# Wider weight-gradient chunks, whole spectral weights and another order of weight transfers in a fused spectral/SwiGLU forward-backward kernel

## Chip, cores and metric

The kernel runs on one core of one Trainium2 chip. The metric is device time in microseconds (us), lower is better. Times are medians over runs; traces are single profiled runs. The engines are called PE (TensorE), DVE (VectorE), ACT (ScalarE), POOL (GpSimd) and SP (SyncE). SP, POOL and ACT start transfers: I call their streams of transfers the sync queue, the software queue (POOL) and the ACT queue.

## The reference

One layer, forward and backward, in bf16 with x of 2048 x 512 (S x D) and F = 1792:

```python
def _A_ref(x, w_r, w_i):
    X = rfft2(x.astype(float32))            # 2048 x 257 complex
    return irfft2(X * (w_r + 1j * w_i), s=(S, D)).astype(bfloat16)

def _B_ref(x, w1, w3, w2):
    return (silu(x @ w1) * (x @ w3)) @ w2

def _fwd_reference(x, w_r, w_i, w1, w3, w2):
    h = x + _A_ref(_layernorm(x), w_r, w_i)
    return h + _B_ref(_layernorm(h), w1, w3, w2)
# outputs: the result, and the gradients of x, w_r, w_i, w1, w3, w2 for grad_out
```

## The kernel before

The transforms are matrix products with tables that the kernel makes itself. The order is: layernorm and the forward transform (`r_pass` with stages A, D, B, then `rt_pass`), eight FFN chunks, forward and backward fused, then the backward transform (`r_pass` over `gh_all`, `rt_pass`), and last the weight gradients (wgrad). A framework turns this text into one instruction order for each engine. It places wgrad matmuls as filler into gaps of the backward transform where buffers allow, and it lays out the memory.

Names used below: U is the buffer that carries a transform's result from stage D to stage B (psA, psD and psB are the matmul sums of its stages); `a` holds the FFN's hidden activations, `gg` and `gu` their gradients, and a_t and g_t are transposed chunks of them; go_all is the output gradient, hn_all the normalized rows; ga_ps and o_ps are sums of the FFN. A transfer lands when its data has arrived; time to landing counts from its issue.

The start, where most weights are transferred:

```python
fcp = wes.enter_context(tc.tile_pool(name="fcp", bufs=2))      # chunk buffers of the FFN
...
for pi in range(4):                                            # spectral weights, 2 of 16 rows each
    nc.gpsimd.dma_start(out=wr_c[:], in_=wr_v[:, 2 * pi:2 * pi + 2, :])
    nc.gpsimd.dma_start(out=wi_c[:], in_=wi_v[:, 2 * pi:2 * pi + 2, :])
nc.sync.dma_start_transpose(out=W['w2T'][:], in_=B_w2)
tmpw = gh_all[:, 0:NFB, :]
nc.sync.dma_start_transpose(out=tmpw, in_=B_w1)
nc.sync.dma_start(out=st['w1T'][:], in_=tmpw)
nc.sync.dma_start_transpose(out=tmpw, in_=B_w3)
nc.sync.dma_start(out=st['w3T'][:], in_=tmpw)
...
xn = sp.tile([P, J, D], BF16, name="xn", tag="bigB")           # U has the same tag: it waits
for hlf in range(2):                                           # until xn has been stored
    ...                                                        # layernorm of 8 of 16 rows
    nc.sync.dma_start(out=st['xn'][:, sl, :], in_=xn[:, sl, :])
...
nc.gpsimd.dma_start(out=W['w1'][:], in_=...)
nc.gpsimd.dma_start(out=W['w3'][:], in_=...)
```

The end: loads of the backward transform, and wgrad with chunks of 256 of the 1792 hidden columns:

```python
wpools = dict(big=tile_pool(name="wbig", bufs=3), res=tile_pool(name="wres", bufs=2),
              op=tile_pool(name="wop", bufs=3), ...)
def w_bwd(kl, br, bi):                                         # every second kl
    nc.gpsimd.dma_start(out=state['xs'][:], in_=st['X'][:, kl0:kl0 + 2, :, :])   # xs_c
    nc.gpsimd.dma_start(out=state['wr'][:], in_=wr_v[:, kl0:kl0 + 2, :])         # wr_c
    nc.gpsimd.dma_start(out=state['wi'][:], in_=wi_v[:, kl0:kl0 + 2, :])         # wi_c
...
def wgrad_phase(..., lq, sq):                                  # lq = nc.sync, sq = nc.gpsimd
    go_all = res.tile([P, J, D], BF16, name="go_all", tag="res")
    sq.dma_start(out=go_all[:], in_=go_v)                      # 2 MB
    for f0 in range(0, F, 256):
        a_t = big.tile([P, J, 256], BF16, name="a_t", tag="big")
        lq.dma_start_transpose(out=a_t[:], in_=st['a'][f0:f0 + 256, :])          # 1 MB
        ...                                                    # 2 x 16 matmuls 128x512, 2 outputs
    hn_all = res.tile([P, J, D], BF16, name="hn_all", tag="res")
    sq.dma_start(out=hn_all[:], in_=st['hn'][:])               # 2 MB
    for key, outw in (('gg', out4), ('gu', out5)):
        for f0 in range(0, F, 256):
            ...                                                # g_t 1 MB, 4 x 16 matmuls 128x256
```

## Time and profile before

| | before |
|---|---|
| time, first 4 runs | 729.88 us median (724.06 to 744.47) |
| time, all 16 runs beside the changed kernel | 739.21 us median (724.06 to 747.71) |
| span of the profiled run | 725.9 us |
| first matmul on U (stage B, forward) | 69.7 us |
| last FFN matmul | 474.8 us |
| last stage-B matmul of the backward transform | 529.6 us |
| last wgrad matmul | 719.8 us |

The profile page of before: busy time of PE in us, its share of the span and the number of its instructions, then some of its rows of 40 equal slices, in tenths of a slice.

```profile
PE 636.7 (88%) x4736; PEld 453.1 (62%) x4736; DVE 435.1 (60%) x1349; ACT 298.2 (41%) x585; POOL 77.0 (11%) x140
PE   0261999989989898999999899979999999999996
PEclk9995998999999999999999999999999999999999
DMA  9998320375506051331506050698510589988881
```

A slice is 18 us. After the fourth slice PE is near full to the end. So time can be won mainly where PE stands, in the first 70 us.

The timeline of before's sync queue (start, time in the queue, instruction):

```profile
1.70 32.53 SPq L610 DMA_TRANSPOSE w2T<-in_B_w_dram  x1
34.27 7.30 SPq L612 DMA_TRANSPOSE gh_all<-in_B_w_dram  x1
...
51.13 6.95 SPq L614 DMA_TRANSPOSE gh_all<-in_B_w_dram  x1
58.18 0.52 SPq L629 DMA_DIRECT2D st_xn<-xn  x1
...
60.59 0.76 SPq L629 DMA_DIRECT2D st_xn<-xn  x1
```

And what U waited for in before (the waits: who waits for what, us in total, times, longest):

```profile
DVE U L72 <- DMA st_xn<-xn: 23.0, 1, 23.0
...
PE psBr L213 <- ACT U L71: 17.8, 1, 17.8
```

The store of xn stands behind three transposes, U waits for the store, PE waits for U. The first transpose took 32.5 us, a later one of the same size 7.3 us.

### The profile page before, as it was taken

The numbers are of one execution on the slowest core, as the hardware profiler recorded it, in microseconds if no ns is written. First come the engines' busy times: TensorE is split into PE (matmuls) and PEld (weight loads), VectorE is DVE, ScalarE is ACT, GpSimd is POOL, SyncE is SP. The second block draws the span as 40 slices with busy tenths as digits, with TensorE's granted clock in tenths as the row PEclk, the third lists the DMA queues.
The fourth block names the chain that finished last, engine by engine and source line by source line (L and its number), as shares of the span: only waits on it lengthen the run. The fifth ranks groups of instructions, "written<-read, shape, count | busy, mean of one in ns | idle before, by whom it ended". The sixth has DMA issues, their size and how long they took to land.

```text
span 725.9 us, 12323 instructions
## 1 busy us (share of the span) xinstructions
PE 636.7 (88%) x4736; PEld 453.1 (62%) x4736; DVE 435.1 (60%) x1349; ACT 298.2 (41%) x585; POOL 77.0 (11%) x140
## 2 busy tenths in 40 slices
PE   0261999989989898999999899979999999999996
PEld 0141987467574746657574748559865444788885
DVE  6940787769393947759493957477986874010010
ACT  1560335566181634537181736354356552000000
POOL 4000310010000000000000000033410222111221
PEclk9995998999999999999999999999999999999999
DMA  9998320375506051331506050698510589988881
GB/s 255 226 280 296 98 79 1 111 244 203 163 30 182 30 167 31 107 90 62 150 31 181 31 166 3 177 252 332 142 50 29 121 189 212 230 178 196 171 193 37
DMA packets 167979, 103.87 MB, mean 143 GB/s; under 512 B 111600, under 2 KB 154608, under 8 KB 166896
## 3 DMA queue, kind: packets, MB, share of 16 engines
q1 hardware_dynamic: 159168, 68.43, 38.9%
q0 software_dynamic: 8464, 33.60, 14.2%
q10 hardware_dynamic: 288, 1.05, 0.4%
q8 instruction: 37, 0.61, 0.3%
q14 instruction: 22, 0.18, 0.1%
HBM read 29.91 MB, written 45.63 MB: 104 GB/s over the span
## 4 chain that ended last, share of the span: by engine, by line
DVE 30%; PE 23%; issue 17%; DMA 13%; SPq 10%; POOL 4%; ACT 2%; POOLq 0%; ACTq 0%; DVEq 0%
SPq L610 4%; DMA h_c<-st_h 4%; PE ps L278 3%; SPq L449 3%; DVE t L422 3%; POOL out_dram L492 3%; SPq L441 3%; DVE ggT L425 3%; DMA gh_all<-in_B_w_dram 3%; DVE aT L418 2%; DVE t L424 2%; DVE guT L426 2%; PE psDr L204 2%; PE psDi L205 2%; PE ghn_ps L446 2%
## 5 line engine op out<-in xcount | busy, mean ns | idle before, releaser
L485 PE MATMUL pw<-g_t,hn_all 128*128 128x256 bf16 x896 | 98.0, 273 | 0.0
L485 PEld LDWEIGHTS <-hn_all 128*128 128x128 bf16 x896 | 87.7, 98 | 10.4
L445 PE MATMUL ghn_ps<-w1T,ggT 128*128 128x512 bf16 x224 | 84.9, 379 | 0.0
L446 PE MATMUL ghn_ps<-w3T,guT 128*128 128x512 bf16 x224 | 84.9, 379 | 0.0
L409 PE MATMUL ga_ps<-goT,w2T 128*128 128x256 bf16 x448 | 67.2, 272 | 11.6 <-ACT th L415 11.6
L405 PE MATMUL g_ps<-hnT,w 128*128 128x256 bf16 x448 | 67.2, 273 | 1.9 <-DVE goT L388 1.9
L407 PE MATMUL u_ps<-hnT,w 128*128 128x256 bf16 x448 | 67.2, 273 | 0.0
L490 DVE CAST o_w<-pw 128x512 bf16<-128x512 f32 x14 | 9.7, 692 | 88.1 <-PE pw L485 88.1
L204 PE MATMUL psDr<-FD,Tt 128*128 128x257 bf16 x256 | 59.7, 279 | 2.1 <-ACT Tt L71 2.1
L205 PE MATMUL psDi<-FD,Tt 128*128 128x257 bf16 x256 | 59.6, 278 | 0.0
L437 PE MATMUL o_ps<-w,aT 128*128 128x512 bf16 x224 | 50.9, 379 | 7.3 <-DVE aT L418 7.3
L409 PEld LDWEIGHTS <-w2T 128*128 128x128 bf16 x448 | 43.8, 98 | 17.7 <-issue 12.7
L466 PE MATMUL pw<-go_all,a_t 128*128 128x512 bf16 x224 | 51.4, 379 | 0.0
L405 PEld LDWEIGHTS <-w 128*128 128x128 bf16 x448 | 43.8, 98 | 8.6 <-issue 2.0
L407 PEld LDWEIGHTS <-w 128*128 128x128 bf16 x448 | 43.8, 98 | 5.1
L488 ACT CAST o_w<-pw 128x512 bf16<-128x512 f32 x14 | 8.2, 585 | 89.6 <-PE pw L485 89.6
L307 DVE BATCH_NORM_STATS2 ln_st<-h_c 128x6 f32<-128x512 bf16 x16 | 10.4, 684 | 52.7 <-DMA h_c<-st_h 52.7
L437 PEld LDWEIGHTS <-aT 128*128 128x128 bf16 x224 | 21.0, 98 | 33.6 <-DVE aT L418 10.7
L191 PE MATMUL psA<-TT,xn 128*128 128x256 bf16 x64 | 11.5, 338 | 34.5 <-DVE xn L329 28.0
L414 ACT ACTIVATE sg<-g_ps 128x512 bf16<-128x512 f32 x56 | 34.7, 619 | 15.3 <-DVE guT L426 8.9
L345 ACT ACTIVATE lb_t<-lb_gsb,lb_ne,rinv_all 128x512 f32<-128x512 f32 x16 | 13.0, 813 | 64.4 <-DVE ln_t L315 34.7
L204 PEld LDWEIGHTS <-Tt 128*128 128x128 bf16 x256 | 37.1, 145 | 3.4 <-ACT Tt L71 2.3
(221 smaller groups left out, 1244.9 us busy)
## 6 DMA issues: line engine op xcount, KB each, us to landing
st_a<-aT SPq DMA_DIRECT2D x8, 896.0 KB, 4.7
st_gg<-ggT SPq DMA_DIRECT2D x8, 896.0 KB, 6.3
st_gu<-guT SPq DMA_DIRECT2D x8, 896.0 KB, 9.0
w<-in_B_w_dram POOLq DMA_DIRECT2D x3, 1792.0 KB, 19.6
out_dram<-o_w POOLq DMA_DIRECT2D x42, 128.0 KB, 3.6
wr_c<-in_A_w_r_dram POOLq DMA_DIRECT2D x16, 128.5 KB, 5.3
wi_c<-in_A_w_i_dram POOLq DMA_DIRECT2D x16, 128.5 KB, 4.0
st_X<-xs_t POOLq DMA_DIRECT2D x8, 257.0 KB, 2.5
```

Source lines behind the costliest of these rows:

```text
L204: nc.tensor.matmul(pr[:, :DF], lhsT=lhsT, rhs=T.FD[:, v_re, dc, :], start=(n == 0), stop=(n == 7))
L205: nc.tensor.matmul(pi[:, :DF], lhsT=lhsT, rhs=T.FD[:, v_im, dc, :], start=(n == 0), stop=(n == 7))
L405: nc.tensor.matmul(g_ps[:, fbi, :], lhsT=W['w1'][:, dc, fs], rhs=hnT[:, dc, :], start=(dc == 0), stop=(dc == 3))
L407: nc.tensor.matmul(u_ps[:, fbi, :], lhsT=W['w3'][:, dc, fs], rhs=hnT[:, dc, :], start=(dc == 0), stop=(dc == 3))
L409: nc.tensor.matmul(ga_ps[:, fbi, :], lhsT=W['w2T'][:, dc, fs], rhs=goT[:, dc, :], start=(dc == 0), stop=(dc == 3))
L414: nc.scalar.activation(out=sg[:], in_=g_ps[:], func=ACT.Silu)
L437: nc.tensor.matmul(o_ps[:], lhsT=aT[:, fb, jj * P:(jj + 1) * P], rhs=W['w2'][:, fb, :], start=(fb == 0), stop=(fb == NFB - 1))
L445: nc.tensor.matmul(ghn_ps[:], lhsT=ggT[:, fb, jj * P:(jj + 1) * P], rhs=W['w1T'][:, fb, :], start=(fb == 0), stop=False)
L446: nc.tensor.matmul(ghn_ps[:], lhsT=guT[:, fb, jj * P:(jj + 1) * P], rhs=W['w3T'][:, fb, :], start=False, stop=(fb == NFB - 1))
L466: nc.tensor.matmul(pw[:], lhsT=a_t[:, j, fbi * P:(fbi + 1) * P], rhs=go_all[:, j, :], start=(j == 0), stop=(j == J - 1))
L485: nc.tensor.matmul(pw[:, dd, :], lhsT=hn_all[:, j, db * P:(db + 1) * P], rhs=g_t[:, j, :], start=(j == 0), stop=(j == J - 1))
L610: nc.sync.dma_start_transpose(out=W['w2T'][:], in_=B_w2)
```

## The change

The intent: let the forward transform start sooner (xn stored before the third weight transpose, fewer and larger loads), and give wgrad fewer, wider steps (512 columns, chunks in four shared 2 MB slots instead of three 1 MB chunk slots and two 2 MB slots). Row-wise gx transfers and a separate pool for the first FFN chunk make the memory fit.

```diff
 def wgrad_phase(...):
-    FW = 256
-    go_all = res.tile([P, J, D], BF16, name="go_all", tag="res")
+    FCH = [(0, 512), (512, 512), (1024, 512), (1536, 256)]
+    go_all = big.tile([P, J, D], BF16, name="go_all", tag="big")
     sq.dma_start(out=go_all[:], in_=go_v)
-    for f0 in range(0, F, FW):
-        a_t = big.tile([P, J, FW], BF16, name="a_t", tag="big")
-        lq.dma_start_transpose(out=a_t[:], in_=st['a'][f0:f0 + FW, :])
+    for ci, (f0, fw) in enumerate(FCH):
+        a_t = big.tile([P, J, 512], BF16, name="a_t", tag="big")
+        lq.dma_start_transpose(out=a_t[:, :, :fw], in_=st['a'][f0:f0 + fw, :])
+        if ci == 1:
+            hn_all = big.tile([P, J, D], BF16, name="hn_all", tag="big")
+            sq.dma_start(out=hn_all[:], in_=st['hn'][:])
 ...                      # outputs in pairs: 23 transfers instead of 42
-    fcp = wes.enter_context(tc.tile_pool(name="fcp", bufs=2))
+    cp0 = wes.enter_context(tc.tile_pool(name="cp0", bufs=1))   # first chunk only; fcp later
 ...
-        for pi in range(4):  ...   # 8 loads of 2 rows, and 8 more later
+        nc.gpsimd.dma_start(out=wr_t[:], in_=wr_v)
+        nc.gpsimd.dma_start(out=wi_t[:], in_=wi_v)
 ...
-        nc.sync.dma_start_transpose(out=tmpw, in_=B_w3)
-        nc.sync.dma_start(out=st['w3T'][:], in_=tmpw)
 ...                      # layernorm, xn stores
+        nc.sync.dma_start_transpose(out=tmpw, in_=B_w3)
+        nc.sync.dma_start(out=st['w3T'][:], in_=tmpw)
+        nc.sync.dma_start(out=W['w1'][:], in_=...)
+        nc.sync.dma_start(out=W['w3'][:], in_=...)
-        nc.gpsimd.dma_start(out=W['w1'][:], in_=...)
-        nc.gpsimd.dma_start(out=W['w3'][:], in_=...)
 ...
-        wpools = dict(big=...bufs=3, res=...bufs=2, op=...bufs=3, ...)
+        wpools = dict(big=...bufs=4, op=...bufs=2, ...)
 ...                      # gx: xnr and gxt row by row; four xs buffers in the forward pass
```

More of the change, by code (lines that the diff above doesn't have):

```diff
@@ L452, in wgrad_phase @@
 def wgrad_phase(nc, grad_out, st, out4, out5, out6, pools, lq, sq):
-    big, res, op, ps = (pools[k] for k in ("big", "res", "op", "ps"))
+    big, op, ps = (pools[k] for k in ("big", "op", "ps"))
     go_v = grad_out.rearrange("(p j) d -> p j d", j=J)
-    FW = 256
+    FCH = [(0, 512), (512, 512), (1024, 512), (1536, 256)]
     k = 0
-    go_all = res.tile([P, J, D], BF16, name="go_all", tag="res")
-    sq.dma_start(out=go_all[:], in_=go_v)
-    for f0 in range(0, F, FW):
-        a_t = big.tile([P, J, FW], BF16, name="a_t", tag="big")
-        lq.dma_start_transpose(out=a_t[:], in_=st['a'][f0:f0 + FW, :])
-        for fbi in range(FW // P):
-            fb = f0 // P + fbi
-            pw = ps.tile([P, D], FP32, name="pw", tag="ps")
-            for j in range(J):
-                nc.tensor.matmul(pw[:], lhsT=a_t[:, j, fbi * P:(fbi + 1) * P], rhs=go_all[:, j, :], start=(j == 0), stop=(j == J - 1))
-            o = op.tile([P, D], BF16, name="o_w", tag="o")
-            if k % 2 == 0:
-                nc.scalar.copy(out=o[:], in_=pw[:])
-            else:
-                nc.vector.tensor_copy(out=o[:], in_=pw[:])
-            k += 1
-            sq.dma_start(out=out6[fb * P:(fb + 1) * P, :], in_=o[:])
@@ L474, in wgrad_phase, with evac @@
-    hn_all = res.tile([P, J, D], BF16, name="hn_all", tag="res")
-    sq.dma_start(out=hn_all[:], in_=st['hn'][:])
+    def evac(o_ap, p_ap):
+        nonlocal k
+        if k % 2 == 0:
+            nc.scalar.copy(out=o_ap, in_=p_ap)
+        else:
+            nc.vector.tensor_copy(out=o_ap, in_=p_ap)
+        k += 1
+    go_all = big.tile([P, J, D], BF16, name="go_all", tag="big")
+    sq.dma_start(out=go_all[:], in_=go_v)
+    hn_all = None
+    out6_v = out6.rearrange("(fb p) d -> p fb d", p=P)
@@ new lines, in wgrad_phase @@
+    for ci, (f0, fw) in enumerate(FCH):
[4 more added lines that the diff above has]
+            sq.dma_start(out=hn_all[:], in_=st['hn'][:])
+        nfb = fw // P
+        for fb2 in range(nfb // 2):
+            o = op.tile([P, 2, 512], BF16, name="o_w", tag="o")
+            for fbi in range(2):
+                fbl = fb2 * 2 + fbi
+                pw = ps.tile([P, D], FP32, name="pw", tag="ps")
+                for j in range(J):
+                    nc.tensor.matmul(pw[:], lhsT=a_t[:, j, fbl * P:(fbl + 1) * P], rhs=go_all[:, j, :], start=(j == 0), stop=(j == J - 1))
+                evac(o[:, fbi, :], pw[:])
+            fbg = f0 // P + fb2 * 2
+            sq.dma_start(out=out6_v[:, fbg:fbg + 2, :], in_=o[:])
@@ L476, in wgrad_phase @@
     for key, outw in (('gg', out4), ('gu', out5)):
-        for f0 in range(0, F, FW):
-            g_t = big.tile([P, J, FW], BF16, name="g_t", tag="big")
-            lq.dma_start_transpose(out=g_t[:], in_=st[key][f0:f0 + FW, :])
+        outw_v = outw.rearrange("(db p) f -> p db f", p=P)
+        for (f0, fw) in FCH:
+            g_t = big.tile([P, J, 512], BF16, name="g_t", tag="big")
+            lq.dma_start_transpose(out=g_t[:, :, :fw], in_=st[key][f0:f0 + fw, :])
             for db2 in range(2):
-                pw = ps.tile([P, 2, FW], FP32, name="pw1", tag="ps")
+                o = op.tile([P, 2, 512], BF16, name="o_w", tag="o")
@@ L482, in wgrad_phase @@
                 for dd in range(2):
                     db = db2 * 2 + dd
+                    pw = ps.tile([P, 512], FP32, name="pw1", tag="ps")
                     for j in range(J):
-                        nc.tensor.matmul(pw[:, dd, :], lhsT=hn_all[:, j, db * P:(db + 1) * P], rhs=g_t[:, j, :], start=(j == 0), stop=(j == J - 1))
-                o = op.tile([P, 2, FW], BF16, name="o_w", tag="o")
-                if k % 2 == 0:
-                    nc.scalar.copy(out=o[:], in_=pw[:])
-                else:
-                    nc.vector.tensor_copy(out=o[:], in_=pw[:])
@@ L491, in wgrad_phase @@
-                k += 1
-                sq.dma_start(out=outw[db2 * 2 * P:(db2 * 2 + 2) * P, f0:f0 + FW].rearrange("(dd p) f -> p dd f", p=P), in_=o[:])
+                        nc.tensor.matmul(pw[:, :fw], lhsT=hn_all[:, j, db * P:(db + 1) * P], rhs=g_t[:, j, :fw], start=(j == 0), stop=(j == J - 1))
+                    evac(o[:, dd, :fw], pw[:, :fw])
+                sq.dma_start(out=outw_v[:, db2 * 2:db2 * 2 + 2, f0:f0 + fw], in_=o[:, :, :fw])
 def bg_weight_transposes(nc, T, W, st, w2nat, psb, stg, dq):
@@ L602 @@
             eng.dma_start(out=xt[:, g4 * 4:(g4 + 1) * 4, :], in_=x_v[:, g4 * 4:(g4 + 1) * 4, :])
-        wch = []
-        for pi in range(4):
-            wr_c = s4.tile([P, 2, DF], BF16, name="wr_c", tag="wr_c")
-            wi_c = s4.tile([P, 2, DF], BF16, name="wi_c", tag="wi_c")
-            nc.gpsimd.dma_start(out=wr_c[:], in_=wr_v[:, 2 * pi:2 * pi + 2, :])
-            nc.gpsimd.dma_start(out=wi_c[:], in_=wi_v[:, 2 * pi:2 * pi + 2, :])
-            wch.append((wr_c, wi_c))
+        wr_t = sp.tile([P, J, DF], BF16, name="wr_t", tag="wr_t")
+        wi_t = sp.tile([P, J, DF], BF16, name="wi_t", tag="wi_t")
+        nc.gpsimd.dma_start(out=wr_t[:], in_=wr_v)
+        nc.gpsimd.dma_start(out=wi_t[:], in_=wi_v)
         nc.sync.dma_start_transpose(out=W['w2T'][:], in_=B_w2)
@@ L629 @@
             nc.sync.dma_start(out=st['xn'][:, sl, :], in_=xn[:, sl, :])
+        nc.sync.dma_start_transpose(out=tmpw, in_=B_w3)
+        nc.sync.dma_start(out=st['w3T'][:], in_=tmpw)
+        nc.sync.dma_start(out=W['w1'][:], in_=B_w1.rearrange("(dc p) f -> p dc f", p=P))
+        nc.sync.dma_start(out=W['w3'][:], in_=B_w3.rearrange("(dc p) f -> p dc f", p=P))
         scrB = sp.tile([P, 8192], I32, name="scrB", tag="bigA")
         gen_tables_FD_KB(nc, T, smc, scrB, io)
-        nc.gpsimd.dma_start(out=W['w1'][:], in_=B_w1.rearrange("(dc p) f -> p dc f", p=P))
-        nc.gpsimd.dma_start(out=W['w3'][:], in_=B_w3.rearrange("(dc p) f -> p dc f", p=P))
         Y = sp.tile([P, J, 2, DF], BF16, name="Y", tag="bigC")
@@ L641, in w_fwd @@
             if kk == 0:
-                state['xs'] = s2.tile([P, 2, 2, DF], BF16, name="xs_t", tag="xs_t")
-                if kl0 // 2 < len(wch):
-                    state['wr'], state['wi'] = wch[kl0 // 2]
-                else:
-                    state['wr'] = s4.tile([P, 2, DF], BF16, name="wr_c", tag="wr_c")
-                    state['wi'] = s4.tile([P, 2, DF], BF16, name="wi_c", tag="wi_c")
-                    nc.gpsimd.dma_start(out=state['wr'][:], in_=wr_v[:, kl0:kl0 + 2, :])
-                    nc.gpsimd.dma_start(out=state['wi'][:], in_=wi_v[:, kl0:kl0 + 2, :])
+                state['xs'] = s4.tile([P, 2, 2, DF], BF16, name="xs_t", tag="xs_t")
+                state['wr'] = wr_t[:, kl0:kl0 + 2, :]
+                state['wi'] = wi_t[:, kl0:kl0 + 2, :]
             xs = state['xs']
@@ L659, in w_fwd @@
                 t2 = s2.tile([P, 2, DF], BF16, name="wt2", tag="wt2")
-                nc.vector.tensor_tensor(out=t1[:], in0=Xr, in1=wr_c[:], op=ALU.mult)
-                nc.vector.tensor_tensor(out=t2[:], in0=Xi, in1=wi_c[:], op=ALU.mult)
+                nc.vector.tensor_tensor(out=t1[:], in0=Xr, in1=wr_c, op=ALU.mult)
+                nc.vector.tensor_tensor(out=t2[:], in0=Xi, in1=wi_c, op=ALU.mult)
                 nc.vector.tensor_tensor(out=Y[:, kl0:kl0 + 2, 0, :], in0=t1[:], in1=t2[:], op=ALU.subtract)
@@ L664, in w_fwd @@
                 t4 = s2.tile([P, 2, DF], BF16, name="wt2", tag="wt2")
-                nc.vector.tensor_tensor(out=t3[:], in0=Xr, in1=wi_c[:], op=ALU.mult)
-                nc.vector.tensor_tensor(out=t4[:], in0=Xi, in1=wr_c[:], op=ALU.mult)
+                nc.vector.tensor_tensor(out=t3[:], in0=Xr, in1=wi_c, op=ALU.mult)
+                nc.vector.tensor_tensor(out=t4[:], in0=Xi, in1=wr_c, op=ALU.mult)
                 nc.vector.tensor_tensor(out=Y[:, kl0:kl0 + 2, 1, :], in0=t3[:], in1=t4[:], op=ALU.add)
@@ L680, in h_cons @@
                 if j0 == 0:
-                    state['h0'] = fcp.tile([P, 2, D], BF16, name="h_c", tag="h_c")
+                    state['h0'] = cp0.tile([P, 2, D], BF16, name="h_c", tag="h_c")
                 state['ht'] = state['h0'] if j0 == 0 else s2.tile([P, 2, D], BF16, name="ht", tag="ht")
@@ L689 @@
         rt_pass(nc, T, Y, sp, ps, h_cons, Evac(nc), Evac(nc), Evac(nc))
-        ch = ffn_prologue(nc, T, st, half, go_v, 0, fcp, sm, s2, ps, rinv2_all, m2_all, h_src=state['h0'])
+        ch = ffn_prologue(nc, T, st, half, go_v, 0, cp0, sm, s2, ps, rinv2_all, m2_all, h_src=state['h0'])
     wpB = wes.enter_context(tc.tile_pool(name="wpB", bufs=1))
@@ L701 @@
         fsm = es.enter_context(tc.tile_pool(name="fsm", bufs=2))
+        fcp = es.enter_context(tc.tile_pool(name="fcp", bufs=2))
         ftp = es.enter_context(tc.tile_pool(name="ftp", bufs=2))
@@ L716 @@
     with ExitStack() as es:
-        wpools = dict(big=es.enter_context(tc.tile_pool(name="wbig", bufs=3)),
-                      res=es.enter_context(tc.tile_pool(name="wres", bufs=2)),
-                      op=es.enter_context(tc.tile_pool(name="wop", bufs=3)),
+        wpools = dict(big=es.enter_context(tc.tile_pool(name="wbig", bufs=4)),
+                      op=es.enter_context(tc.tile_pool(name="wop", bufs=2)),
                       ps=es.enter_context(tc.tile_pool(name="wps", bufs=2, space=PSUM)))
@@ L779, in gx_cons @@
                 j0 = j - jj
-                if jj == 0:
-                    state['xnr'] = s2.tile([P, 2, D], BF16, name="xnr", tag="xnr")
-                    nc.gpsimd.dma_start(out=state['xnr'][:], in_=st['xn'][:, j0:j0 + 2, :])
-                    state['gxt'] = s2.tile([P, 2, D], BF16, name="gxt", tag="gxt")
-                ln_bwd_row(nc, sm, fpool, pso[:], state['xnr'][:, jj, :], rinv1[:, j:j + 1], gh_all[:, j, :],
-                           state['gxt'][:, jj, :], use_pool=False)
-                if jj == 1:
-                    nc.gpsimd.dma_start(out=out1_v[:, j0:j0 + 2, :], in_=state['gxt'][:])
+                xnr = s4.tile([P, D], BF16, name="xnr", tag="xnr")
+                nc.gpsimd.dma_start(out=xnr[:], in_=st['xn'][:, j, :])
+                gxt = s2.tile([P, D], BF16, name="gxt", tag="gxt")
+                ln_bwd_row(nc, sm, fpool, pso[:], xnr[:], rinv1[:, j:j + 1], gh_all[:, j, :], gxt[:], use_pool=False)
+                nc.gpsimd.dma_start(out=out1_v[:, j, :], in_=gxt[:])
             rt_pass(nc, T, GX, sp, ps, gx_cons, Evac(nc), Evac(nc), Evac(nc))
```

## The prediction

> **What bounds the kernel now.** The span is 725.9 us. The table of stretches shows TensorE (PE) near full after 70 us: 100% busy at 70-100 us, 93-95% in the FFN (180-470 us), 100% at 540-718 us; but 15.6 us of the first 70. The wgrad phase is bound by matmul streaming: by the view of one source line, the w1/w3-gradient matmuls (128x256) come 94 in 10 us, 106 ns each; the w2-gradient ones (128x512) 48 in 10 us, 208 ns each. So 256 columns already stream at the full rate.
>
> The hole at the start waits for one buffer. The chain of waits shows the sync queue holding the w2 transpose (1.7-34.2 us), the w1 transpose (9.4), the w1T store (7.4), the w3 transpose (9.0), and only then the store of xn (8.6). U shares a buffer with xn, so its evictions wait for that store: by the waits, VectorE 23.0 us, PE 17.8 us. PE does two steps of stage D at 48.1-51.8 us, stands until 69.7 us, and comes back cold: matmuls last 0.42 us instead of 0.27 until 74.6 us, granted clock 0.5. The Trainium skill ("TensorE: Matmul & The Clock Gate", Part 1) says an idle array falls to half rate until about 3.4 us of sustained work; the trace agrees, 4.9 us here.
>
> **What the change does.**
> 1. The w3 transpose goes behind the xn stores. The w1/w3 loads (1.8 MB each, issued at 9.8-11.3 us beside the w2 transpose) follow it on the sync queue; the spectral weights come as two 1 MB loads. The w2 transpose took 32.5 us, the w1 one of the same size 7.3: contention, so I expect the w2 transpose done by 20-28 us. Then xn's second half, computed at 39.5 us, is stored by 46-50 us, and U is written from 49 us. PE does 320 matmuls at 0.11 us from 48.1 us and ends near 84 us instead of 104: about -20 us if the wait vanishes, -14 us if half a store stays; all on the critical path.
> 2. wgrad: 896 matmuls of 256 columns become 384 of 512 and 128 of 256; by the measured rates about the same time. Weight loads (98 ns) halve but were hidden.
> 3. Larger chunks cost a bubble. The four big slots hold the gradient, hn and two chunks; the first gg chunk gets its slot only when the third a chunk is used up. Its 2 MB transpose, estimated from the 1.83 MB one (9.4 us to landing), takes 10-12 us; the last a chunk gives PE only 32 x 0.21 = 6.8 us. PE stands 4-5 us, perhaps returning cold: +4 to +7 us. Later chunks have three slots and 13.6 us of work each.
> 4. Four xs buffers, row-wise gx transfers, the first FFN chunk's own pool, 23 output DMAs instead of 42: off the path, within 1 us.
>
> **Sum.** -19 + 5 = -14 us on a median of 729.88: about 715; I lean a little lower, 714, range 704 to 724. Faster by over 2% 0.57, within 2% 0.39, slower 0.04.
>
> **What would show it.** VectorE's wait for the xn store under 6 us; no PE hole at 52-69 us, no half clock at 70-75; the forward transform's end 14-20 us earlier; FFN chunks unchanged at 40.4 us; wgrad at 208 ns per 512 columns; one PE wait of 3-6 us before the first gg matmul.
>
> **What would make it wrong.** A scheduler orders each queue; it may still put the w3 transpose ahead of the xn store: then the gain is near 0. The w2 transpose may be slow by itself, so that the xn store leaves late. The bubble may be hidden if a chunks finish early as filler, or repeat if 2 MB transposes take over 13.6 us.

## The result, and the profile after

The changed kernel is correct and slower: 770.87 us median (762.38 to 778.42, 11 runs), against 739.21 us for before (16 runs). The ratio is 1.056, with a 95% interval of 1.049 to 1.064. A ratio is always the mean time of one kernel's fast runs over that of before's fast runs of the same rounds, so it isn't quite the ratio of the quoted medians. Most of before's own runs fall into two groups, 724 to 728 us and 736 to 748 us; some of the slower ones were sorted out as slow, depending on the fastest run of their batch. A ratio can therefore move by a per cent between batches, and I read no smaller difference across batches.

The page of the changed kernel, the same rows as before:

```profile
PE 641.4 (83%) x4352; PEld 417.2 (54%) x4352; DVE 434.2 (56%) x1351; ACT 298.7 (39%) x587; POOL 65.6 (9%) x121
PE   0279999849999989999999997009999999699897
PEclk9979999989999999999999999558999999899999
DMA  9992104825060605141423248997610286968941
```

PE's work is nearly the same (641.4 and 636.7 us), so the loss is standing time. There is a new hole of two slices (19 us each) near 490 us, in which the DMA row reads 9, and two new dips (at the ninth slice and near the end). The granted clock reads half (5) in the hole itself. Milestones, read from the traces, place the difference of the spans, 42.6 us (more than the 31.7 us between the medians, since before's trace is one of its quicker runs):

| event on PE | before, us | after, us | difference, summed | this step |
|---|---|---|---|---|
| first FFN matmul | 156.0 | 140.6 | -15.4 | -15.4 start |
| first o_ps matmul (first chunk's tail) | 175.2 | 174.4 | -0.8 | +14.6 first chunk |
| last FFN matmul | 474.8 | 468.0 | -6.8 | -6.0 given back in later chunks |
| last stage-B matmul, backward | 529.6 | 563.7 | +34.1 | +40.9 the hole |
| last a matmul | 621.8 | 654.7 | +32.9 | -1.2 |
| first gg matmul | 622.0 | 661.5 | +39.5 | +6.6 slot |
| last wgrad matmul | 719.8 | 763.2 | +43.4 | +3.9 output buffers |
| end | 725.9 | 768.5 | +42.6 | -0.8 |

The changed kernel's waits, the lines that answer to those of before and the new ones of PE:

```profile
DVE U L72 <- DMA st_xn<-xn: 9.1, 1, 9.1
...
PE pw L483 <- DMA a_t<-st_a: 39.0, 2, 38.7
...
PE pst L384 <- DVE hn_c L329: 9.5, 1, 9.5
...
PE pw L498 <- DMA g_t<-st_gg: 6.5, 1, 6.5
...
PE psBr L213 <- ACT U L71: 2.2, 1, 2.2
PE pw L498 <- ACT o_w L461: 2.1, 1, 2.1
```

**The start.** The timeline of the changed kernel's sync queue:

```profile
1.69 16.32 SPq L615 DMA_TRANSPOSE w2T<-in_B_w_dram  x1
18.05 7.21 SPq L617 DMA_TRANSPOSE gh_all<-in_B_w_dram  x1
...
33.08 0.33 SPq L632 DMA_DIRECT2D st_xn<-xn  x1
38.25 11.23 SPq L633 DMA_TRANSPOSE gh_all<-in_B_w_dram  x1
49.58 0.52 SPq L632 DMA_DIRECT2D st_xn<-xn  x1
```

The w2 transpose fell to 16.3 us. The scheduler still put the w3 transpose ahead of the second half of xn, so DVE still waits 9.1 us for the store instead of 23.0 (under 6 was predicted). PE's wait for U fell from 17.8 to 2.2 us, and stage B starts at 55.8 instead of 69.7 us.

**The first FFN chunk.** PE's timeline of the changed kernel (start, duration of the group, instruction, idle time before it and what ended that):

```profile
162.69 0.60 PE L409 MATMUL ga_ps<-goT,w2T 128*128 128x256 bf16 x4
172.76 0.29 PE L384 MATMUL pst<-ident,hn_c 128*128 128x128 bf16 x1 [9.47 <-DVE hn_c L329]
...
174.44 5.84 PE L437 MATMUL o_ps<-w,aT 128*128 128x512 bf16 x24
```

Between the first chunk's two halves stand the transposes of the *second* chunk's normalized rows. PE's compiled order puts them ahead of the first chunk's output matmuls, and in the trace PE stood 9.47 us for those rows: their `h_c` load, issued at 140.7 us, landed 16.4 us later, while three weight loads of 1.8 MB, issued on the software queue from 138.0 us, were under way.

**The hole.** Three lines from the timelines of before, its SP and POOL queues:

```profile
467.57 15.94 SPq L461 DMA_TRANSPOSE a_t<-st_a  x3
...
480.03 0.54 POOL L741 DMA_DIRECT2D xs_c<-st_X  x1 [323.88 <-DVE gh_all L352]
...
489.08 0.53 POOL L458 DMA_DIRECT2D go_all<-in_grad_out_dram  x1
```

The same of the changed kernel:

```profile
468.42 58.67 SPq L472 DMA_TRANSPOSE a_t<-st_a  x2
...
468.65 1.07 POOL L741 DMA_DIRECT2D xs_c<-st_X  x2 [328.43 <-PE ghn_ps L446]
469.71 0.53 POOL L467 DMA_DIRECT2D go_all<-in_grad_out_dram  x1
```

Time from issue to landing of the a_t transposes at that place, first in before (three of 1 MB):

```profile
DMA to landing us min/median/max: 7.0/8.9/10.3
```

and in the changed kernel (two of 2 MB):

```profile
DMA to landing us min/median/max: 15.7/33.1/50.6
```

In before, the software queue's first load stood until 480.0 us; the trace names a DVE instruction on `gh_all` as its releaser, so I take it that the load's buffer lay where that instruction's data had been. When `go_all` was issued at 489.1 us, the first three transposes had landed. In the changed kernel the releaser named is another instruction (PE `ghn_ps`), and both go at 468.7 to 469.7 us, right beside the transposes. The overlap was not written anywhere; that it follows from the layout is read from these releasers. `go_all` took 39.9 us to land instead of 8.3.

Busy time in stretches, before: columns are the stretch, its length, PE, weight loads, DVE, ACT, POOL (us busy and instructions), granted clock, DMA share, GB/s.

```profile
468.00:485.00 17.00, 13.48 (x74) 7.93 (x73) 9.98 (x19) 7.68 (x15) 4.24 (x8) 0.90 1.10 234
485.00:510.00 25.00, 23.41 (x201) 21.20 (x199) 20.15 (x53) 11.61 (x31) 9.22 (x18) 1.00 0.91 314
```

The same stretches of the changed kernel:

```profile
468.00:485.00 17.00, 8.21 (x60) 5.57 (x58) 10.95 (x19) 9.36 (x18) 5.32 (x10) 0.93 1.03 165
485.00:510.00 25.00, 0.00 (x0) 0.00 (x0) 0.00 (x0) 0.00 (x0) 0.00 (x0) 0.50 1.20 76
```

From 485 to 510 us every compute engine stands. The DMA engines count as busy over their whole time (1.20) and move 76 GB/s, where they move 314 in before. A full DMA share therefore doesn't mean that much is moved. By the view of the DMA queues, the transposes' 256-byte packets alone account for 0.91 of the 1.20: 1597 packets in these 25 us, 229 ns each (0.913 x 16 engines x 25 us / 1597). In before, at 468 to 485 us, 12815 packets of that queue took 22 ns each (105.4%). So each packet of the transposes took ten times as long; why is not shown.

### The profile page after: what moved, and what is told of

The parts are those of the page before. It is cut to its first block, busy times and chain, and to the rows that moved or that the text cites. A ratio compares the mean times of both kernels' runs of the same rounds, so it can differ in the third digit from the quotient of the medians.

```text
span 768.5 us, 11527 instructions
## 1 busy us (share of the span) xinstructions
PE 641.4 (83%) x4352; PEld 417.2 (54%) x4352; DVE 434.2 (56%) x1351; ACT 298.7 (39%) x587; POOL 65.6 (9%) x121
## 4 chain that ended last, share of the span: by engine, by line
PE 43%; DVE 25%; DMA 14%; SPq 7%; another core or an unknown queue 5%; ACT 3%; issue 3%; POOLq 0%; ACTq 0%; DVEq 0%
PE pw L498 12%; DMA h_c<-st_h 5%; PE ps L278 3%; PE pw L483 3%; PE o_ps L437 3%; PE ghn_ps L446 2%; PE ghn_ps L445 2%; SPq L615 2%; DVE t L422 2%; PE psDr L204 2%; DVE ggT L425 2%; DMA a_t<-st_a 2%; SPq L441 2%; PE psDi L205 2%
## 5 line engine op out<-in xcount | busy, mean ns | idle before, releaser
L498 PE MATMUL pw<-g_t,hn_all 128*128 128x512 bf16 (+1 forms) x512 | 99.9, 359 | 8.6 <-DMA g_t<-st_gg 6.5
L483 PE MATMUL pw<-go_all,a_t 128*128 128x512 bf16 x224 | 53.4, 384 | 40.0 <-DMA a_t<-st_a 39.0
L498 PEld LDWEIGHTS <-hn_all 128*128 128x128 bf16 x512 | 50.6, 99 | 58.0 <-issue 12.8
L463 DVE CAST o_w<-pw 128x512 bf16<-128x512 f32 (+1 forms) x23 | 14.8, 643 | 110.4 <-PE pw L498 93.5
L204 PE MATMUL psDr<-FD,Tt 128*128 128x257 bf16 x256 | 61.6, 285 | 2.1 <-ACT Tt L71 2.1
L205 PE MATMUL psDi<-FD,Tt 128*128 128x257 bf16 x256 | 61.4, 284 | 0.0
L483 PEld LDWEIGHTS <-a_t 128*128 128x128 bf16 x224 | 21.4, 99 | 64.7 <-DMA a_t<-st_a 39.7
L461 ACT CAST o_w<-pw 128x512 bf16<-128x512 f32 (+1 forms) x23 | 12.5, 545 | 112.2 <-PE pw L498 94.9
L72 DVE CAST Tt<-psA 128x512 bf16<-128x512 f32 x26 | 16.6, 685 | 40.7 <-PE psA L191 40.3
```

The source lines that it names most:

```text
L204: nc.tensor.matmul(pr[:, :DF], lhsT=lhsT, rhs=T.FD[:, v_re, dc, :], start=(n == 0), stop=(n == 7))
L205: nc.tensor.matmul(pi[:, :DF], lhsT=lhsT, rhs=T.FD[:, v_im, dc, :], start=(n == 0), stop=(n == 7))
L483: nc.tensor.matmul(pw[:], lhsT=a_t[:, j, fbl * P:(fbl + 1) * P], rhs=go_all[:, j, :], start=(j == 0), stop=(j == J - 1))
L498: nc.tensor.matmul(pw[:, :fw], lhsT=hn_all[:, j, db * P:(db + 1) * P], rhs=g_t[:, j, :fw], start=(j == 0), stop=(j == J - 1))
```

## The experiments

Two theories stood at the outset. **Order:** PE's compiled order has the first wgrad matmul ahead of the last six stage-A matmuls of the backward transform (it is PE's matmul 2939 instead of 3262), so a late chunk blocks the transform. **Contention:** transposes and software-queue loads in flight together crawl, whatever PE's order is. A third question was whether the pieces other than wgrad cost anything.

### Parts of the change: `start_fcp`, `bwd_only`

```diff
 # start_fcp: the changed kernel
-    wgrad 512, gx row-wise, pools of after          # undone: all as before
 # bwd_only: the kernel before
+    wgrad 512, gx row-wise, pools of after          # done alone
```

> The changed kernel with the whole backward part (wgrad chunks, its pools, row-wise gx transfers) as before; the start and the first FFN chunk's own pool as changed. Theory: the start gains 14 to 16 us up to the first FFN matmul, the first FFN chunk loses 8 to 15 us of it, and the 38.7 us hole near 480 us is absent, because the first wgrad matmul stands behind the whole backward transform again in PE's order: about 7 us faster than before, ratio 0.98 to 1.00. Rival (the changed start is itself what costs): ratio above 1.02.

Measured: 739.07 us, 1.012 [1.002, 1.022], slower than expected. The start gained as in the full change (stage B at 56.8 us), but the first chunk lost it (first FFN matmul to first o_ps 33.6 us, 19.2 in before), and PE had a wait of 17.6 us for U in the backward transform: with wgrad *unchanged*, `go_all` now started beside the 1 MB transposes, and one took 43.1 us to land. From the last FFN matmul to the end this trace is 15.5 us longer than before's.

> The kernel before with only the backward part changed (512-column wgrad chunks, four big slots, row-wise gx transfers). In its compiled order the gradient load stands again behind the first spectral loads, and the first wgrad matmul behind the backward transform. Theory A (the hole comes of an order of instructions that only the whole change produces, together with a slow transpose): no hole of 38 us; left are the slot bubbles at the first gg chunk and at the output buffers, 6 to 15 us: ratio 1.01 to 1.02. Rival B (2 MB transposes are slow by themselves, so wgrad as changed costs all): a PE wait of over 30 us on the first transposed chunk, ratio over 1.045.

Measured: 774.96 us, 1.061 [1.042, 1.080]. No single 38 us wait came (the longest there was 10.3 us), so neither theory held as put. But a_t landed after up to 38.4 us with PE's order as in before. The time is as long as the whole change's, but not from wgrad alone: the traced run also drew a bad start. The same first queue entry, the w2 transpose, took 47.2 us, and stage B began at 85.5 us. Of the 45.0 us by which this trace is longer than before's, 13.5 are there by the last FFN matmul and 31.5 come after it; in the full change 49.4 come after it.

### PE's order: `order_fix`

```diff
+            with tc.issue_after(last_d):      # after the last stage-D matmul of the transform
                 wgrad_phase(...)
```

> The changed kernel with one added ordering edge: wgrad's PE instructions come after the last stage D matmul of the backward transform. DMA queues keep their order, so the 2 MB gradient load still runs beside the first 2 MB transpose and that transpose should still take about 50 us. Theory A (a slow transpose hurts because one wgrad matmul stands in front of the transform's last six in PE's in-order queue): most of the 38.7 us comes back, PE goes on with the transform; 735 to 755 us, as the spectral loads are slowed by the same contention. Rival C (the contention alone stalls the stage, the order doesn't matter): still a hole of 30 us or more, 763 us or more.

Measured: 765.97 us, 1.044 [1.027, 1.062]; about 5 us less than the changed kernel, and the intervals overlap, so no gain is shown. The waits moved from the wgrad matmul to stage B (30.5 us for U), because what the transform itself needs comes through the same stalled DMA engines. a_t took up to 45.1 us. The order theory falls as the main cause.

### Smaller packets: `go_pieces`

```diff
-    sq.dma_start(out=go_all[:], in_=go_v)
+    for jg in range(4):
+        sq.dma_start(out=go_all[:, jg * 4:(jg + 1) * 4, :], in_=go_v[:, jg * 4:(jg + 1) * 4, :])
```

> The changed kernel with the 2 MB gradient load cut into four of 512 KB on the same software queue, so its packets are 4 KB instead of 16 KB. PE's order keeps the wgrad matmul in front of the last six of the transform. Theory D (it is the large packets of the software queue that starve the 256-byte packets of the transpose): the first transpose lands within 10 to 20 us instead of 50.6 and the hole shrinks to under 10 us: 730 to 745 us. Rival E (any load beside a transpose slows it, whatever its packet size): hole 30 us or more, 760 us or more.

Measured: 751.74 us, 1.030 [1.018, 1.042]. PE's wait for a_t fell from 38.7 to 18.5 us, although PE's order and the bytes were the same. The load goes in packets of 4 KB per partition instead of 16 KB. The Trainium skill ("DMA: Bandwidth & Descriptors", "Queues, rings and completion order") says that a DMA engine alternates between its queues packet by packet; a shorter turn for the load fits that, but the probe below, where 1 KB pieces were the slowest, doesn't bear it out. It isn't the whole either: a_t still took up to 31.4 us.

### The overlap by itself: `micro`

A program that runs only a transpose of w1 (1.83 MB) with one kind of load beside it. Its output is wrong, which doesn't matter for the time.

```python
nc.sync.dma_start_transpose(out=X[:, 0, 0:NFB, :], in_=B_w1)
nc.gpsimd.dma_start(out=G, in_=go_v)        # and variants: 4 KB and 1 KB pieces, ACT queue, two loads
```

> A measurement by itself, its outputs are wrong on purpose (zeros). The w1 transpose of the kernel (1.83 MB, 256-byte packets, sync queue) one at a time, each beside another load: alone; beside a 2 MB gradient load on the software queue in 16 KB, 4 KB or 1 KB packets; beside the same load on ScalarE's hardware queue in 16 KB packets; after that load on the same queue; beside a w1 load on the software queue; beside two gradient loads; the loads alone. Theory D (packet size decides, whichever queue): alone 9 to 10 us; 16 KB packets 25 us or more on both queues; 4 KB 12 to 20; 1 KB under 14. Rival F (only the software queue does it): the hardware queue's 16 KB load leaves the transpose under 16 us, the software queue's 16 KB over 25. Rival G (plain bandwidth sharing): every pairing takes about the sum of the two alone, 14 to 18 us.

Measured, transpose from issue to landing: alone 8.6 to 9.0 us; beside the 2 MB software load 14.0 to 19.8; with 4 KB pieces 14.5, with 1 KB pieces 21.3; beside the same load on the ACT queue 14.1 to 14.5; beside two software loads 18.9; beside a software load of w1 14.2. The load alone took 7.3 to 7.6 us, so a fair share would give about 16.6 us (the sum). In isolation this is plain sharing with some unfairness. The crawl to 40 and more us wasn't reproduced. Packet size alone and queue alone don't explain it.

### Moving loads to other queues: `after_gohn`, `after_hwq`, `after_nosw`

```diff
 # after_gohn: the changed kernel
-    sq.dma_start(out=go_all[:], in_=go_v)
+    lq.dma_start(out=go_all[:], in_=go_v)              # sync queue; the same for hn_all
 # after_hwq: also
-        nc.gpsimd.dma_start(out=wr_t[:], in_=wr_v)
+        nc.scalar.dma_start(out=wr_t[:], in_=wr_v)     # ACT queue; the same for wi_t
 # after_nosw: after_gohn, and
-                    nc.gpsimd.dma_start(out=state['xs'][:], in_=...)
+                    nc.scalar.dma_start(out=state['xs'][:], in_=...)   # also wr, wi, xnr
```

> The changed kernel with the gradient and hn loads of wgrad on the sync queue, in line with the transposes instead of beside them on the software queue (PE's order thereby returns to wgrad behind the transform). Theory: no hole at 480 to 519 us, the first transpose lands within 25 us of its issue though behind a 2 MB load, PE goes on through the transform; the slot bubbles at 620 to 660 and 707 us stay (about 15 us). 725 to 740 us. Rival B (a 2 MB transpose is slow by itself): the transpose takes over 30 us from issue to landing.

Measured: 755.39 us, 1.029 [1.011, 1.048]. go_all now lands in 8.9 us, but a_t still takes up to 40.0 us: the small loads of the backward transform, with packets near 4 KB, are still on the software queue beside it. I had expected 725 to 740; the large load was not the only partner.

> As after_gohn, and the two 1 MB spectral loads at the start on ScalarE's hardware queue. Under rival F (software queue) the w2 transpose takes under 12 us instead of 16.3, and the whole start is not slower than in after_gohn; under theory D (packet size) it stays near 16 us. Time as after_gohn, within 5 us, since the second xn store is held by the w3 transpose's place in the queue either way.

Measured: 757.08 us, 1.035 [1.022, 1.048], no gain over after_gohn; the w2 transpose still takes 16.2 us. At the start the queue of the spectral loads doesn't matter.

> after_gohn with the other loads of the backward stage (stored spectrum, spectral weights, xn rows; 128 to 257 KB each) also taken off the software queue, to ScalarE's hardware queue. Theory F2 (a transpose and loads of the software queue in flight together crawl, whatever the size; hardware-queue loads only share bandwidth): both first 2 MB transposes land within 16 us of their issue instead of 26 to 40, PE's waits for U in the backward transform (18.7 us in all in after_gohn) fall under 6 us: 730 to 742 us. Rival H (any small loads, or the 2 MB transposes by themselves, make it slow): transposes still over 25 us, no gain over after_gohn's 755.

Measured: 744.2 us, 1.021 [1.014, 1.029]. With no load on the software queue beside them, a_t landed after at most 21.2 us (16 was expected), and PE's wait for U there was 5.8 us. The ratio is within a per cent of after_gohn's, so I read no gain in time. The Trainium skill ("DMA: Bandwidth & Descriptors", "Issuing engines are not separate DMA queues") says that transfers of all engines run on the same 16 DMA engines. That agrees with the ACT queue not being free of cost (14.1 us instead of 9.0 in the probe); but the landing of the transposes fell from 40.0 to 21.2 us here. The queue and the timing aren't separated in this: on the ACT queue the weight loads also started later (first at 482.4 us, 475.0 in after_gohn).

### Taking the overlap away: `after_hoist`, `after_clear`

These keep the changed kernel's widths, queues and bytes. `after_hoist`, the control, writes the first two a_t transposes ahead of the backward transform in the text, so that others can refer to them (PE's order becomes that of order_fix). `after_clear` lets each first load of the software queue depend on both transposes by a one-element write into its target:

```diff
+            def gate(one):
+                nc.gpsimd.tensor_tensor(out=one, in0=pre['a'][0][0:1, 0, 0:1],
+                                        in1=pre['a'][1][0:1, 0, 0:1], op=ALU.add)
+            gate(pre['go'][0:1, 0, 0:1])          # likewise for the first xs_c, wr_c, wi_c and xnr
```

> Control for after_clear: the changed kernel with its first two transposes of the a-gradient written ahead of the backward transform in the program, so that another instruction can name them; TensorE's order is then again the one in which the wgrad matmuls do not stand in front of the transform. The loads on the software queue start beside the transposes as before. Both theories expect about what order_fix showed: 1.03 to 1.06 of the kernel before, the slowest a-transpose landing after 35 us or more.

> The same, but each of the first loads of the software queue (gradient, spectra, spectral weights, normalized rows) is made to wait until both first a-transposes have landed, by a one-element write into its target that reads both. If the overlap of transposes and loads is the cause of the hole, the transposes land within 9 to 14 us, no wait of TensorE at 480 to 530 us is over 12 us, and the time falls by 20 to 35 us against after_hoist (to 1.00 to 1.02 of before), although the loads start some 15 us later. If the size of the transposes alone is the cause (rival), they still take 25 us or more; if the later loads cost what the overlap cost, the time stays within 8 us of after_hoist.

Measured, on the same chip: after_hoist 779.78 us, 1.056 [1.044, 1.068]; after_clear 750.92 us, 1.020 [1.008, 1.031]. From the timeline, the tile view and the waits of after_hoist:

```profile
472.13 68.73 SPq L738 DMA_TRANSPOSE a_t<-st_a  x2
...
DMA to landing us min/median/max: 19.2/42.1/65.0
...
PE psBr L214 <- DVE U L72: 38.6, 5, 34.5
```

The same of after_clear:

```profile
468.36 15.99 SPq L738 DMA_TRANSPOSE a_t<-st_a  x2
...
DMA to landing us min/median/max: 10.5/10.8/11.1
...
PE psBr L214 <- DVE U L72: 16.9, 5, 10.4
```

With the overlap gone, the transposes take 16.0 instead of 68.7 us in the queue, and the time falls by 29 us, although every load starts later. This settles that the overlap, not the size of the transposes, makes them slow and makes most of the hole. It doesn't bring all of it back: from the last FFN matmul to the last a matmul it is 147.0 us in before, 193.4 in after_hoist and 166.6 in after_clear. So 26.8 us came of the overlap and 19.6 remain, with 16.9 us of waits for U in them; the loads now start later, and the 2 MB hn load was issued ahead of the small spectral loads (488.7 and 489.2 us), an order whose removal in best2_wgrad2 below went with 14 us less. Two 2 MB transposes in 16.0 us are 8.0 us each; the 261 GB/s that the Trainium skill gives for a transpose with a non-contiguous middle dimension ("DMA: Bandwidth & Descriptors", "Latency and other measured facts") would make 2.1 MB / 261 GB/s = 8.0 us, an estimate that the trace agrees with (I didn't check that this transpose is of that kind).

### The start, rightly ordered: `before_queues`, `best2`, `best2_again`

```diff
 # before_queues: the kernel before, wgrad of 256 columns
-            nc.gpsimd.dma_start(out=wr_c[:], in_=...)     # first 8 spectral loads
+            nc.scalar.dma_start(out=wr_c[:], in_=...)
-        nc.gpsimd.dma_start(out=W['w1'][:], in_=...)
+        with tc.issue_after(st_xn.ins):                   # behind both xn stores
+            nc.sync.dma_start(out=W['w1'][:], in_=...)    # w3 likewise
-    sq.dma_start(out=go_all[:], in_=go_v)
+    lq.dma_start(out=go_all[:], in_=go_v)                 # hn_all likewise; order edge of order_fix
 # best2: also
+        with tc.issue_after(st_xn.ins):
+            nc.sync.dma_start_transpose(out=tmpw, in_=B_w3)
```

> The kernel before, wgrad and FFN untouched, with only queues changed: w1 and w3 loads on the sync queue behind the xn stores, the first eight spectral loads on ScalarE's hardware queue, wgrad's gradient and hn loads on the sync queue behind the first three transposes, and the ordering edge that keeps wgrad's matmuls behind the transform. Theory: the w2 transpose takes 8 to 12 us instead of 32.5, the xn stores leave by 41 us, U is written by 50 us, PE's wait of 17.8 us at the start is under 5 us: 705 to 715 us in the profile, ratio 0.96 to 0.98. Rival (the start's gain is given back later, as in start_fcp): ratio 0.99 or more.

Measured: 717.1 us, 0.983 [0.978, 0.989], just short of what was expected. The w2 transpose takes 18.7 us, not 8 to 12, the w3 transpose still stands ahead of the xn stores (46.7 and 49.1 us, not by 41), PE waits 6.7 us for U, and stage B starts at 59.9 us. a_t lands in 6.8 to 9.8 us.

> before_queues with the w3 transpose and the w1 and w3 loads all behind both xn stores on the sync queue. The xn stores leave at 33 to 41 us, U is written from 49 us: PE's wait for U (6.7 us there) goes under 2 us and the first U matmul comes at about 50 to 52 instead of 59.9 us: 5 to 9 us under before_queues, 706 to 712 us. Rival (w3T or the weights then come late for the FFN): no gain.

Measured: 707.16 us, 0.971 [0.965, 0.976], 5 rounds: faster than both kernels. The sync queue of best2:

```profile
1.69 17.98 SPq L610 DMA_TRANSPOSE w2T<-in_B_w_dram  x1
22.57 6.89 SPq L612 DMA_TRANSPOSE gh_all<-in_B_w_dram  x1
...
32.73 7.61 SPq L627 DMA_DIRECT2D st_xn<-xn  x2
40.39 9.55 SPq L631 DMA_TRANSPOSE gh_all<-in_B_w_dram  x1
```

Here both xn stores really precede the w3 transpose; PE no longer waits for U at the start, and stage B starts at 51.4 us.

> The best version again, on the same chip as best2_wgrad2, for a direct comparison: 704 to 709 us, 0.965 to 0.976 of before.

Measured: 708.7 us. No ratio could be formed in this batch, as all but one of before's seven runs counted as slow.

### The pool of the first chunk: `bq_fcp`

```diff
 # before_queues with
-    fcp = wes.enter_context(tc.tile_pool(name="fcp", bufs=2))
+    cp0 = wes.enter_context(tc.tile_pool(name="cp0", bufs=1))   # first chunk; fcp among the FFN's pools
```

> before_queues with only the first FFN chunk's own pool, as the change has it. Theory: the move lets two chunks' prologues be scheduled early, VectorE's order puts the second hn behind the whole first chunk and PE stands in front of the transposes: first FFN matmul to first output matmul grows from 19.3 to 28 us or more, PE waits about 9 us for hn, of which some comes back later: 4 to 12 us over before_queues' 717. Rival: no difference (within 3 us), then the loss in the first chunk came of the loads moved at the start.

Measured: 735.15 us, 1.009 [1.003, 1.016], where before_queues had 0.983: about 18 us dearer (735.15 - 717.1). PE waits 10.4 us for hn_c, and from the first FFN matmul to o_ps it takes 39.7 us instead of 19.3. In the traces 15.9 us of the 20.7 us between the two spans are there by the last FFN matmul. The rest of the loss is in the backward transform, where the layout had shifted too: go_all took 15.3 us and a_t up to 20.4. The direction was expected, the size was not.

### Wide wgrad on the good start: `bq_wgrad_nosw`, `best2_wgrad`, `best2_wgrad2`

```diff
 # bq_wgrad_nosw: before_queues + wgrad 512 + gx row-wise + backward loads on the ACT queue
 # best2_wgrad:   best2 + wgrad 512 + gx row-wise + the gates of after_clear
 # best2_wgrad2:  best2_wgrad, with
-    sq.dma_start(out=go_all[:], in_=go_v)
+    lq.dma_start(out=go_all[:], in_=go_v)     # sync queue, behind the two transposes; hn_all too
```

> before_queues with the changed wgrad (512-column chunks, four slots) and row-wise gx transfers, and the backward stage's loads on hardware queues: the price of the chunks in a clean place. Theory: only the bubbles named in the prediction and the output buffers are left, 6 us before the first gg chunk and 2 to 5 us for two output buffers instead of three; against before_queues' 717 it is 720 to 732 us. Rival B: the large chunks cost by themselves 20 us or more.

Measured: 752.75 us, 1.033 [1.026, 1.040]; far off 720 to 732. ACT, whose instruction stream now held these loads beside its copies to U, waited 14.8 us before one of those copies and held up PE (PE's wait for U there 12.7 us); a_t took up to 25.4 us, and the first gg chunk cost 6.7 us. The remedy brought its own trouble.

> The best version (start in the right order) with the wide wgrad chunks, row-wise gx transfers and the waiting loads of after_clear. If widening by itself costs only the slot bubble (about 7 us), the two-buffer output wait (about 4 us) and what is left of the overlap, the time is 0.98 to 1.00 of before, 7 to 18 us over best2 (0.9706). If widening is worse by something else, it is over 1.01.

Measured: 746.46 us, 1.014 [1.006, 1.022], 39 us over best2's 707.16, expected 7 to 18. Of PE's waits, 23 us (U 12.0, gy_t 11.0) lay at 485 to 510 us: my gates had put the 2 MB hn load ahead of the small spectral loads.

> best2_wgrad left 39 us against best2, where 7 to 18 were expected; 23 us of its waits lay at 485 to 510 us, where the small spectral loads stood behind the 2 MB hn load on the software queue. Here the gradient and hn come on the sync queue behind the first two transposes, and only the small loads wait for the transposes. If that wait was the experiment's own fault, the time falls to 718 to 730 us (0.98 to 0.995 of before) and the waits there are under 10 us together; the first gg wait (6 us) and the output waits (2 to 4 us) stay. If the two wide transposes with what must follow them are too much for the DMA engines in any order (rival), the waits stay over 15 us and the time over 735 us.

Measured: 732.72 us beside best2_again's 708.7 us on the same chip. The ratio of the means is 732.46 / 708.56 = 1.034, from four fast runs each; 24 us. I expected 718 to 730, so it is just missed, nearer to the first theory. PE's new waits in the trace of best2_wgrad2:

```profile
PE psBr L214 <- DVE U L72: 9.8, 5, 8.5
PE pw L486 <- DVE o_w L463: 4.5, 1, 4.5
PE pw L501 <- DMA g_t<-st_gg: 3.7, 1, 3.7
PE pw L486 <- DMA go_all<-in_grad_out_dram: 3.4, 1, 3.4
PE pw L501 <- ACT o_w L461: 3.0, 1, 3.0
```

They sum to 24.4 us, near the 26.8 us between the spans of the two traces; in best2_again none of these lines exceeds 2 us. So wide chunks, with the gates and the row-wise gx transfers, cost about 24 us in this kernel even with start and overlap in order: 3.7 for the slot, 7.5 for two output buffers instead of three, 13.2 for U and the gradient (under 10 was expected), which I put down to loads that now stand behind 4 MB of transposes instead of 3. Without a run of best2 with the gates alone, the price of the width by itself isn't shown.

## Why the prediction was wrong, point by point

**What bounds it: right. Step 1 (start, -14 to -20 us): right in size, in part by luck.** It came to -15.4 us at the first FFN matmul. The order that the step rests on didn't come about: the scheduler put the w3 transpose before the second xn store, for which the prediction had said "the gain is near 0". The gain came all the same, because the w2 transpose took 16.3 us instead of 32.5 in the queue and left it at 18.0 us, where 20 to 28 was predicted. best2 shows what forcing the order gives: stage B at 51.4 instead of 55.8 us.

**Step 2 (wgrad streams at the same rate): right.** 512-column matmuls come 48 in 10 us in the trace, 208 ns each, and PE's busy time hardly changed. By the same fact widening had nothing to win: weight loads halved, but were hidden.

**Step 3 (slot bubble +4 to +7 us): right.** PE waited 6.5 us for the first gg chunk (3.7 to 6.7 us in the other wide versions).

**Step 4 failed: "Four xs buffers, row-wise gx transfers, the first FFN chunk's own pool, 23 output DMAs instead of 42: off the path, within 1 us."** Three terms were missing in it.
- *The hole, +40.9 us.* The step counted changed buffers by their own work and did not ask when their transfers would start. The prediction had the cost in hand, for step 1 puts the 32.5 us of the w2 transpose down to the loads beside it, but step 3 took 10 to 12 us for a 2 MB transpose, from an undisturbed one, and no step asked what would run beside wgrad's first. In before, the software queue's loads were held by a buffer until 480.0 us; in the changed kernel they went at 468.7 us, beside the first 2 MB transposes, which then took up to 50.6 us to land (the 1 MB ones of before 7.0 to 10.3). after_clear against after_hoist shows this cause (29 us for removing the overlap alone; about 20 us of the loss in this part remained there, with the loads behind the transposes). start_fcp shows that even 1 MB transposes are hit when the layout makes them overlap, so wide chunks aren't a condition. Why the engines crawl at 76 GB/s in the kernel while an isolated pair merely shares (14 to 20 us) stays open; packet size may have a part in it (go_pieces), the queue or the timing of its loads another (after_nosw), and neither is all.
- *The first chunk's own pool, +14.6 us, of which 6.0 came back.* It changed when weights and second-chunk rows arrive; PE stood 9.5 us before transposes placed ahead of ready work. bq_fcp shows the direction by itself, at about 18 us; its layout side effects in the backward transform are in that number.
- *Two output buffers, +3.9 us.* Outputs landed beside a 2 MB transpose, and ACT found no free buffer; PE's wait was 2.1 us and the rest of the gap cold matmuls or slowed streaming, which I didn't separate.

**The sum.** Predicted -19 + 5 = -14. Measured -15.4 + 8.6 + 40.9 - 1.2 + 6.6 + 3.9 - 0.8 = +42.6 us, in the two profiled runs.

**My first explanation fell too.** PE's order, which the wait line names (wgrad matmul waiting for a_t), gave back about 5 us at most when repaired, which is within the noise.

**Before's two groups of times** were a trap for a prediction on four runs. The start's first transpose took 32.5 us in one trace and 47.2 us in another kernel with the same start, moving stage B by 15.8 us. That fits the gap between the groups, but no trace of before in its slower group was taken, so it is argued, not shown. In the batch of best2, six of before's eleven runs lie between the groups (731 to 735 us), so two groups are a rough picture.

## What to carry to other kernels

Ask of every buffer that a change moves or frees which transfer it held back, and what that transfer will run beside; where an overlap must not happen, write the order down instead of leaving it to the memory layout. Read the DMA share together with GB/s: 1.20 busy at 76 GB/s was a jam here; the same engines moved 314 GB/s in before. Where matmuls already stream at their full rate, as here (106 ns for 256 columns, 208 for 512), wider chunks win nothing, but larger transfers, fewer slots and fewer output buffers each added a wait. The gain that was there lay in the order of the start's transfers: the weight loads behind the xn stores (before_queues, 0.983), then the w3 transpose too (best2, 0.971).

## What the Trainium skill lacked or had wrong

- "DMA: Bandwidth & Descriptors", section "Rules for kernel authors": "A transpose next to ordinary DMAs needs nothing". The row is about corruption, and there all runs that should be right agree. It says nothing of time: a 2 MB transpose beside software-queue loads landed after up to 65.0 us, and after 11.1 us without them.
- No page that I read gives the slowdown of a transpose beside loads. In isolation, 1.83 MB: 9.0 us alone, 14.0 to 19.8 us beside a 2 MB software load, 21.3 us when that load goes in 1 KB pieces. The kernel's further slowdown isn't explained by these.
- "DMA: Bandwidth & Descriptors", section "Issuing engines are not separate DMA queues": right that the queues share the engines, but it has the choice of queue save only issue time. Moving the backward loads from the software queue to the ACT queue went with a fall of the slowest a_t landing from 40.0 to 21.2 us; part of that may be the loads' later start.
- "TensorE: Matmul & The Clock Gate", Part 1: agrees that an idle array falls to half rate. The granted clock fell to 0.50 in the hole, and the first matmuls after it took 0.62 us instead of 0.38. The half clock lasted 4.9 us of work at the start of before, longer than the about 3.4 us of sustained work that the page names.
